# Decode attention with a gated mixer, one core: the main rows of wq requested ahead of its tail, and a root of a constant on ScalarE ahead of the request for x

## The chip, the cores and the metric

The kernel runs on one core of one Trainium2 chip. The metric is the device time of one execution in microseconds (us); lower is better. Times inside an execution are us from the start of the profiled span, and the engines are called as in the profile: PE (TensorE), DVE (VectorE), ACT (ScalarE), POOL (GpSimd), SP (SyncE, which here only requests transfers).

## What is computed

One token of width 448 passes through an attention over a cache of 65536 keys and values, and through a small mixer; a gate blends the two. All inputs are bf16.

```python
D, Hq, Hkv, Sk, Dh, F = 448, 16, 8, 65536, 256, 1792
g = sigmoid((x * gate_w).sum(-1, keepdims=True))
q = (x @ wq).reshape(1, 1, Hq, Dh)                  # wq is [448, 4096]
p = softmax(q . k_cache * Dh ** -0.5)               # two query heads share one of 8 cache heads
a = (p . v_cache).reshape(1, 1, Hq * Dh) @ wo
h = (x - mean(x)) / sqrt(var(x) + 1e-5)
b = gelu(h * w1 + b1) contracted with w2, + b2      # a table of F hidden values for each of D
out = g * a + (1 - g) * b
```

The two caches are 268 MB each. Everything else that is read is under 8 MB.

## The kernel before

**The stream.** The caches are read in 32 blocks (8 heads, 4 blocks of 16384 positions each). A block of keys is 8.39 MB and so is a block of values. A loop with two blocks in each pass handles blocks 0 to 29, and straight code after it handles the last two. Keys lie in `k_all`, which has three slots of half a block; values lie in the single tile `vt`. All large transfers are requested by SP, one after the other, by `load_k_whole` (L132), `load_v` (L135), `load_wo_wide` (L144) and, at the end, `load_v_last`. SP waits in front of a request until its target is free: for the keys of the next block until DVE has transposed the slot (L410), for values until PE has used up the block before (L438). For each block DVE transposes eight pieces of keys, PE multiplies them with the queries (`scores`, L418), the softmax follows, and PE multiplies the weights with the values (`pv`).

**The opening.** Ahead of the loop the queries are made from wq, the mixer is computed as far as its contraction, and constants are built. wq lies for that time in `vt`, where values come later: its rows 0 to 383 as `wq_m` (3 rows to a partition, 3072 KB, called the main rows below), its rows 384 to 447 as `wq_t` (half a row to a partition, 512 KB, the tail). Each column of q takes four matmuls, three with main rows (L299) and one with the tail (L306), so the fourth matmul of 128 needs the tail. The chain of the mixer is: x (`xr`) is spread over the partitions by PE (L245), DVE takes mean and variance (L266 to L269), ACT the root (L272), DVE refines its reciprocal (L275 to L282) and normalises (L283), ACT computes 14 GELUs (L288), PE contracts them (L352). The tables w1, b1, w2 are turned by PE in L263, and DVE copies the result (L273) ahead of the reciprocal. The gate's sum is taken by DVE (L346, L347), and its exponential by ACT (L348). DVE finishes the mixer (L357 to L368), which stands behind the loop in the text and is placed ahead of it by the build. Then all engines meet, and the loop begins: PE spreads a slice of wo and ends a head (L563, L540, L554), DVE adds (L558) and begins to transpose the keys.

**What sets the order.** `seq` fixes the order of instructions on each engine to that of the program's text. Two queues carry transfers: SP's and ACT's. On ACT's queue stand x, the three tables, the gate's weights in two halves, and b2, in this order, ahead of ACT's arithmetic. On SP's queue stand the tail of wq, its main rows and block 0 of the keys.

**The counters.** The build gives each transfer one of eight completion counters, in turn. A transfer that gets a counter which an earlier transfer holds is not requested before that one has landed, and what stands behind it on its queue waits too. Before the change they are: x 0, tail 1, tables 2 to 4, main rows 5, gate halves 6 and 7, b2 again 0 (it waits for x), keys of block 0 again 1 (they wait for the tail).

Of the kernel before, what the change touches and what calls it, by code (L numbers as in the profile page):

```python
# [8 lines left out]
FP32 = mybir.dt.float32  # L9
BF16 = mybir.dt.bfloat16  # L10
ACT = mybir.ActivationFunctionType
# [22 lines left out]
def kernel(  # L34
# [15 lines left out]
    nc = tc.nc  # L50
# [12 lines left out]
    def seq(ins):  # L63
        e = ins.ins.engine
        if e in last:
            tc.add_manual_dep(
                ins.ins,
                last[e],
                mybir.DependencyInfo(
                    mybir.DependencyClass.NoSync, mybir.DependencyReason.DATA  # L70
                ),
                reason="program order",
            )
        last[e] = ins.ins.name
        return ins

    kvpool = ctx.enter_context(tc.tile_pool(name="kvpool", bufs=1))
    const = ctx.enter_context(tc.tile_pool(name="const", bufs=1))
# [26 lines left out]
    xr = const.tile([1, D], BF16)  # L105
# [4 lines left out]
    DM = 384  # L110
    wq_m = vt[:, 0:48, :].rearrange("p a b -> p (a b)").rearrange("p (k n) -> p k n", k=3)
# [47 lines left out]
    def load_v_last(n):  # L159
# [3 lines left out]
                in_=rows("v", n)[:, j0:j1, :],  # L163
            ))

    seq(nc.scalar.dma_start(out=xr[:], in_=A_x[0, 0].rearrange("(o n) -> o n", o=1)))
    seq(nc.sync.dma_start(
        out=wq_t[:, :], in_=A_wq[DM:D, :].rearrange("r (h n) -> (r h) n", h=2)
    ))
    seq(nc.sync.dma_start(out=wq_m, in_=A_wq[0:DM, :].rearrange("(p k) n -> p k n", k=3)))  # L170
    for k, table in enumerate((
        B_w1[0].rearrange("(b p) -> b p", p=128),
        B_b1.rearrange("(b p) -> b p", p=128),
# [3 lines left out]
    for n0, n1 in ((0, D // 2), (D // 2, D)):  # L177
        seq(nc.scalar.dma_start(
            out=gw[:, n0:n1], in_=gate_w.rearrange("(o n) -> o n", o=1)[:, n0:n1]
# [14 lines left out]
        out=val[:], in_=rowsel[:, :, :, 0:NI], op=ALU.add, axis=AXIS.XY  # L194
    ))
    fst = const.tile([128, 2, REP], FP32)
    for e in range(2):
        seq(nc.vector.tensor_reduce(
            out=fst[:, e, :], in_=rowsel[:, :, :, e:e + 1], op=ALU.add, axis=AXIS.XY
# [3 lines left out]
        out=par[:], in_=ident_f[:].rearrange("p (a r) -> p r a", r=REP), op=ALU.add, axis=AXIS.X  # L203
# [3 lines left out]
        out=nval[:], in0=val[:], scalar1=-scale, scalar2=None, op0=ALU.mult  # L207
# [7 lines left out]
        out=same[:], in_=val[:].unsqueeze(1).to_broadcast([128, 64, REP])  # L215
# [8 lines left out]
        out=sel[:],  # L224
        in_=ident.rearrange("p (w k) -> p w k", w=NW).unsqueeze(2).to_broadcast([128, NW, NQ, 32]),
# [7 lines left out]
        out=xrr[:], in_=xr[:, DM:D].unsqueeze(2).to_broadcast([1, D - DM, 2])  # L233
    ))
    x_col = hd_ps[:, 40:44]
    for k in range(3):
# [13 lines left out]
        out=xtm[:], in0=par[:], scalar1=x_col[:, 3:4], scalar2=None, op0=ALU.mult  # L250
# [19 lines left out]
        out=veps[:], in0=mv[:, 1:2], scalar1=1e-5, scalar2=None, op0=ALU.add  # L270
# [5 lines left out]
    for _ in range(2):  # L276
# [3 lines left out]
            out=ntmp[:], in0=ntmp[:], scalar1=-0.5, scalar2=1.5, op0=ALU.mult, op1=ALU.add  # L280
# [3 lines left out]
        out=h_bc, in0=xf, scalar1=mv[:, 0:1], scalar2=rstd[:, 0:1],  # L284
        op0=ALU.subtract, op1=ALU.mult,
    ))
    for b in range(NF):
        seq(nc.scalar.activation(  # L288
            out=gel[b], in_=h_bc, func=ACT.Gelu_apprx_tanh,
# [33 lines left out]
    for k in range(2):  # L323
        seq(nc.vector.tensor_copy(
            out=qq[:, :, :, k, :], in_=qq_ps.rearrange("p (w g r) -> p w g r", g=HKV, r=REP)
# [314 lines left out]
    for n in (L - 1, L):  # L640
# [14 lines left out]
        else:  # L655
            def rest_base():
# [9 lines left out]
                out=lsv[:], in0=val[:], scalar1=lsum[:, 0:1], scalar2=None, op0=ALU.mult  # L666
# [8 lines left out]
                out=rdv[:], in0=rdv[:], scalar1=gcol[:, 0:1], scalar2=None, op0=ALU.mult  # L675
# [6 lines left out]
    for c in range(2):  # L682
# [9 lines left out]
        out=oT[:], in0=o_last, in1=rdv[:].unsqueeze(1).to_broadcast([128, 2, REP]), op=ALU.mult  # L692
# [43 lines left out]
```

## Time and profile before

| what | value |
|---|---|
| device time, median of 3 runs (lowest, highest) | 1264.28 us (1263.87, 1925.72) |
| span of the profiled execution | 1261.8 us |
| moved in the span | 544.36 MB, mean 431 GB/s |
| PE, DVE, ACT busy | 824.5, 711.8, 75.7 us |
| ACT busy in the first of 40 slices of the span | 4 tenths; none in any later slice |

Of the profiled execution the page gives its span; what lies around it is not recorded, and the median of the runs is 2.5 us above the span. A row of the timeline gives start and duration in us, engine, line, operation, tiles, count, and in brackets the idle time of the engine before it and what ended that. SPq and ACTq mark what the sequencers of SP and ACT do, such as requests for transfers. A row of the table by stretches gives the stretch, its length, then for PE, PE's weight load, DVE, ACT and POOL the busy time and the count, then the granted clock of PE, the share of the 16 DMA engines that was busy, and GB/s. Packets are put to the stretch in which they begin, so the share of a short stretch can be over 1.

### The profile page before, as it was taken

What the parts mean: (1) busy time and instruction counts of PE and PEld (TensorE: products, weight loads), DVE (VectorE), ACT (ScalarE), POOL (GpSimd) and SP (SyncE); (2) the same over time, 40 slices, a digit from 0 to 9 for tenths busy, and PEclk for the clock granted to TensorE, in tenths of its full rate; (3) what the DMA queues carried; (4) which work ended last, traced back from release to release, by engine and by line L of the source; (5) the groups of instructions that cost most, each with busy time, mean ns of one, the idle gap of its engine ahead of it and who ended that gap; (6) DMA issues with size and microseconds to landing.
All of it is one profiled execution on the core that took longest, in us unless ns stands there. A gap on an engine that the chain in (4) does not pass through costs nothing.

```text
span 1261.8 us, 12358 instructions
## 1 busy us (share of the span) xinstructions
PE 824.5 (65%) x4818; PEld 331.2 (26%) x4818; DVE 711.8 (56%) x755; ACT 75.7 (6%) x163; POOL 4.8 (0%) x9
## 2 busy tenths in 40 slices
PE   4757467575666756577566766658656576665668
PEld 2222122222222312223222322223222232222224
DVE  5665456654556644566544665445655456654575
ACT  4000000000000000000000000000000000000000
POOL 1000000000000000000000000000000000000000
PEclk8887788877787877978778887788877797877878
DMA  9999999999999999999999999999999999999998
GB/s 415 435 435 432 439 432 432 437 434 437 432 434 435 434 425 440 416 441 443 423 434 437 432 432 439 432 439 432 432 439 432 439 432 432 439 432 435 421 435 355
DMA packets 11624, 544.36 MB, mean 431 GB/s; under 512 B 1532, under 2 KB 1918, under 8 KB 2782
## 3 DMA queue, kind: packets, MB, share of 16 engines
q1 hardware_dynamic: 11522, 544.22, 99.6%
q8 instruction: 6, 0.10, 0.0%
q14 instruction: 4, 0.03, 0.0%
q10 hardware_dynamic: 92, 0.01, 0.0%
HBM read 544.22 MB, written 0.00 MB: 431 GB/s over the span
## 4 chain that ended last, share of the span: by engine, by line
DMA 67%; PE 14%; DVE 13%; issue 4%; ACT 0%; SPq 0%; DVEq 0%; ACTq 0%
DMA k_all<-in_A_k_cache_dram 67%; PE sc L418 13%; DVE kT L410 13%; PE hd_ps L463 0%; PE pv_last L438 0%; PE pv_last L563 0%; PE f L563 0%; DVE rmax L475 0%; PE hd_ps L684 0%; ACT p_sb L506 0%; PE hd_ps L554 0%; PE pv_ps L438 0%; PE f L697 0%; PE sm_ps L493 0%; DVE pT L513 0%
## 5 line engine op out<-in xcount | busy, mean ns | idle before, releaser
L418 PE MATMUL sc<-kT,qz 128*128 128x512 bf16 x2048 | 550.4, 419 | 315.0 <-DVE kT L410 314.8
L410 DVE STREAM_TRANSPOSE kT<-k_all 128x2048 f32<-128x2048 f32 x256 | 571.3, 2283 | 207.6 <-DMA k_all<-in_A_k_cache_dram 154.7
L418 PEld LDWEIGHTS <-qz 128*128 128x128 bf16 x2048 | 212.5, 104 | 651.3 <-issue 474.8
L438 PE MATMUL pv_ps<-vt,pT 128*4 128x512 bf16 x1968 | 172.0, 525 | 27.3 <-DVE pT L513 27.3
L519 DVE SCALAR_TENSOR_TENSOR acc<-acc,al,pv_ps 128x512 f32<-128x512 f32 x31 | 23.2, 747 | 160.4 <-PE pv_ps L438 160.4
L438 PEld LDWEIGHTS <-pT 128*4 128x4 bf16 x2000 | 56.5, 108 | 130.1 <-issue 83.9
L506 ACT ACTIVATE p_sb<-sc,nb 128x512 bf16<-128x512 f32 x32 | 22.0, 687 | 1020.0 <-DVE nb L502 1020.0
L475 DVE TENSOR_REDUCE rmax<-sc 128x1 f32<-128x512 f32 x32 | 22.1, 692 | 63.7 <-PE sc L418 63.7
L513 DVE STREAM_TRANSPOSE pT<-p_sb 128x512 bf16<-128x512 bf16 x32 | 22.8, 712 | 27.1 <-ACT p_sb L506 27.1
L525 PE MATMUL hd_ps<-lsum,same 128*128 128x1 f32 x30 | 8.2, 342 | 28.8 <-DVE lsum L514 28.8
L493 PE MATMUL sm_ps<-mrun,ones_f 1*128 1x2 f32 x64 | 12.1, 256 | 21.2 <-DVE mrun L492 13.0
L479 PE MATMUL sm_ps<-ident_f,rmax 128*1 128x128 f32 x32 | 8.6, 270 | 24.5 <-DVE rmax L475 24.5
L563 PE MATMUL pv_last<-wo_in,steps 128*128 128x448 bf16 x64 | 15.6, 368 | 5.5 <-PEq L605 5.5
L563 PEld LDWEIGHTS <-steps 128*128 128x128 bf16 x128 | 11.6, 101 | 22.6 <-issue 14.4
L493 PEld LDWEIGHTS sm_ps<-mrun,ones_f 1*128 1x128 f32 x64 | 9.4, 182 | 27.4 <-DVE mrun L492 16.3
L567 ACT CAST wo_sb<-pv_last 128x448 bf16<-128x448 f32 x16 | 8.5, 532 | 126.3 <-PE pv_last L563 126.3
L558 DVE TENSOR_TENSOR a_acc<-a_acc,hd_ps 1x448 f32<-1x448 f32 x15 | 9.1, 608 | 12.3 <-PE hd_ps L554 12.3
L554 PE MATMUL hd_ps<-wo_sb,oT 128*1 128x448 bf16 x60 | 15.8, 351 | 0.0
L563 PE MATMUL f<-wo_in,steps 128*128 128x448 bf16 x64 | 15.5, 367 | 0.0
L570 ACT COPY wo_sb<-wo_sb 128x896 bf16<-128x896 bf16 x15 | 14.1, 937 | 14.5 <-PE hd_ps L554 14.5
L525 PEld LDWEIGHTS hd_ps<-lsum,same 128*128 128x128 f32 x30 | 6.9, 285 | 30.1 <-DVE lsum L514 30.1
L550 DVE CAST oT<-hd_ps 128x2 bf16<-128x2 f32 x15 | 2.4, 160 | 20.8 <-PE hd_ps L540 20.8
(124 smaller groups left out, 194.6 us busy)
## 6 DMA issues: line engine op xcount, KB each, us to landing
k_all<-in_A_k_cache_dram SPq DMA_DIRECT2D x2, 4096.0 KB, 15.2
vt<-in_A_v_cache_dram SPq DMA_DIRECT2D x1, 5120.0 KB
k_all<-in_A_v_cache_dram SPq DMA_DIRECT2D x1, 4096.0 KB
wo_in<-in_A_wo_dram SPq DMA_DIRECT2D x15, 224.0 KB, 27.8
vt<-in_A_wq_dram SPq DMA_DIRECT2D x1, 3072.0 KB, 10.4
vt<-in_A_v_cache_dram SPq DMA_DIRECT2D x1, 3072.0 KB
k_all<-in_A_v_cache_dram SPq DMA_DIRECT2D x1, 2048.0 KB
k_all<-in_A_v_cache_dram SPq DMA_DIRECT2D x1, 1024.0 KB, 21.7
```

The costliest lines, as they stand in the source:

```text
L410: seq(nc.vector.transpose(out=kT_tiles[i % 2][:].rearrange("p j w k c -> p (j w k c)").bitcast(FP32), in_=slots[pair[i // 4]][:, i % 4 * N ...
L418: seq(nc.tensor.matmul(sc_tiles[e][:, :], lhsT=qz[:, 2 * w + c, 2 * (NI - i):2 * (NI - i) + 128], rhs=kT_tiles[i % 2][:, :, w, :, c], star ...
L438: seq(nc.tensor.matmul(dst[32 * grp:32 * grp + 2 * REP, :, :], lhsT=pT[:, 32 * jj + 2 * REP * ip:32 * jj + 2 * REP * (ip + 1)], rhs=pairs( ...
L475: seq(nc.vector.tensor_reduce(out=rmax[:], in_=sc_ps[:, :], op=ALU.max, axis=AXIS.X))
L493: seq(nc.tensor.matmul(sm_ps[:, 128:128 + REP], lhsT=ones_f[0:1, :], rhs=mrun[0:1, :], start=True, stop=True))
L506: seq(nc.scalar.activation(out=p_sb[:, :], in_=sc_ps[:, :], func=ACT.Exp, scale=scale, bias=nb[:, 0:1], accum_out=den[:, 0:1],))
L513: seq(nc.vector.transpose(out=pT[:, :], in_=p_sb[:, :]))
L519: seq(nc.vector.scalar_tensor_tensor(out=acc[:], in0=acc[:], scalar=al_tiles[e][:, 0:1], in1=src[:, :, :], op0=ALU.mult, op1=ALU.add,))
L525: seq(nc.tensor.matmul(hd_ps[:, 460:461], lhsT=same[:].rearrange("p a r -> p (a r)"), rhs=lsum[:, 0:1], start=True, stop=True,))
L554: seq(nc.tensor.matmul(a_ps, lhsT=oT[:, c, r:r + 1], rhs=wo_sb[:, r, c, :], start=(r == 0 and c == 0), stop=(r == REP - 1 and c == 1),))
L563: seq(nc.tensor.matmul(wo_ps[c], lhsT=steps[:, WS - u:WS - u + 128], rhs=wo_in[:, 2 * u + c, :], start=(u == 0), stop=(u == WS - 1),))
L570: seq(nc.scalar.copy(out=wo_sb[:, 0], in_=wo_sb[:, 1]))
```

## The change

The request for the main rows goes ahead of that for the tail on SP. On ACT, a root of a constant 1.0 is taken ahead of the first request; DVE sets the constant, as its first instruction.

```diff
-    seq(nc.scalar.dma_start(out=xr[:], in_=A_x[0, 0].rearrange("(o n) -> o n", o=1)))
+    seq(nc.sync.dma_start(out=wq_m, in_=A_wq[0:DM, :].rearrange("(p k) n -> p k n", k=3)))
     seq(nc.sync.dma_start(
         out=wq_t[:, :], in_=A_wq[DM:D, :].rearrange("r (h n) -> (r h) n", h=2)
     ))
-    seq(nc.sync.dma_start(out=wq_m, in_=A_wq[0:DM, :].rearrange("(p k) n -> p k n", k=3)))
+    warm = const.tile([1, 1], FP32)
+    seq(nc.vector.memset(warm[:], 1.0))
+    seq(nc.scalar.activation(out=warm[:], in_=warm[:], func=ACT.Sqrt))
+    seq(nc.scalar.dma_start(out=xr[:], in_=A_x[0, 0].rearrange("(o n) -> o n", o=1)))
     for k, table in enumerate((
```

In the built program ACT's first load of the root's table moves with the new root to the head of ACT's instructions, and no load is left ahead of L272. The number of table loads stays three. The counters come out as: main rows 0, x 1, tables 2 to 4, gate halves 5 and 6, b2 7, tail again 0, keys of block 0 again 1. So the first three requests of SP stand like this, with what each waits for:

```
before                                        after
tail of wq                                    main rows of wq
main rows of wq                               tail of wq         [waits for counter 0: the main rows]
keys of block 0 [waits for counter 1: tail]   keys of block 0    [waits for counter 1: x]
```

All other instructions of PE, DVE, POOL and SP keep their order.

## The prediction

> **What bounds the kernel now.** I read the page's head first, then the table by stretches, then the chain of waits, and last the timeline of the opening, where the change lies.
>
> ```profile
> span 1261.8 us, 12358 instructions
> DMA  9999999999999999999999999999999999999998
> ...
> 51.00:1200.00 1149.00, 746.72 (x4201) 296.24 (x4199) 636.68 (x653) 57.92 (x134) 0.00 (x0) 0.81 1.00 434
> 1200.00:1250.00 50.00, 39.11 (x198) 15.09 (x201) 38.85 (x28) 1.41 (x4) 0.00 (x0) 0.85 1.00 431
> 1250.00:1261.80 11.80, 8.96 (x206) 6.10 (x194) 3.33 (x9) 0.85 (x4) 0.00 (x0) 0.75 0.60 244
> ```
>
> All 16 DMA engines are busy from the opening until some 5 us before the end: share 1.00 and 434 GB/s over 1149 us, 1.00 and 431 over the next 50. No compute engine comes near (PE 746.72 of 1149). So the time is the bytes at 434 GB/s, plus what comes before the first byte and after the last. A stop in that stream is made up nowhere; an engine's delay costs something only if a request then comes after the queue has run dry.
>
> The chain of waits shows the same link as a latency, and must not be read as one:
>
> ```profile
> 43.98 26.68 DMA k_all<-in_A_k_cache_dram
> ...
> 0.74 0.42 SPq L167 DMA_DIRECT2D vt<-in_A_wq_dram  x1
> ...
> 1.22 0.41 SPq L170 DMA_DIRECT2D vt<-in_A_wq_dram  x1
> ...
> 3.98 0.33 SPq L132 DMA_DIRECT2D k_all<-in_A_k_cache_dram  x1
> 27.07 0.35 SPq L135 DMA_DIRECT2D vt<-in_A_v_cache_dram  x1
> ...
> vt<-in_A_v_cache_dram SPq DMA_DIRECT2D x1, 24.3
> ...
> DMA to landing us min/median/max: 26.7/27.4/28.1
> ```
>
> The last row is of the key requests in the first 60 us: there are two, and the one at 43.98 has the 26.68, so the one at 3.98 has the 28.1 and block 0 lands at 32.1. The values requested at 27.07 land at 27.07 + 24.3 = 51.4. The keys requested at 43.98 land at 70.7; their 8.39 MB take 8.39 / 0.434 = 19.3 us, and 51.4 + 19.3 = 70.7. So they did not travel for 26.68 us, they stood in line behind the values for 7.4 of them. Requests in the loop have about 7 us of slack.
>
> **The change part by part. The tail's wait on SP.** Tail and main rows were asked for back to back, and the keys as soon as the tail had landed, with the main rows still on their way. Now the tail waits for the main rows, through counter 0, and the keys stand behind it on SP. When the main rows have landed nothing large is queued, and the DMA engines stand still until the tail's first bytes.
>
> ```profile
> vt<-in_A_wq_dram SPq DMA_DIRECT2D x1, 3072.0 KB, 10.4
> ...
> vt<-in_A_wq_dram SPq DMA_DIRECT2D x1, 512.0 KB, 3.2
> ...
> 1.50:1.75 0.25, 0.00 (x0) 0.00 (x0) 0.00 (x0) 0.00 (x0) 0.25 (x1) 1.00 0.01 4
> 1.75:2.00 0.25, 0.00 (x0) 0.00 (x0) 0.00 (x0) 0.00 (x0) 0.23 (x1) 1.00 0.61 213
> ...
> 4.00:5.00 1.00, 0.00 (x0) 0.00 (x0) 1.00 (x1) 1.00 (x1) 1.00 (x1) 1.00 0.96 397
> ...
> 6.00:7.00 1.00, 0.22 (x3) 0.13 (x2) 0.89 (x5) 0.00 (x0) 0.00 (x0) 1.00 0.98 397
> ```
>
> The tail, requested at 0.74, took 3.2 us. Its 0.524 MB at 434 GB/s are 1.2 of them, so 2.0 are fixed: about 1.0 to the first bytes (share 0.01 up to 1.75, 0.61 after), the rest from the last byte to the landing. Before, main rows and tail had both landed at 1.22 + 10.4 = 11.6. Now the main rows are asked for at 0.74 and have no tail ahead of them, so they land 1.2 earlier, at 10.4; the tail is asked for then and lands 3.2 later, at 13.6. That is 2.0 later for the same bytes. The keys are asked for one request behind (1.22 - 0.74 = 0.5), at 10.9; their first bytes would be there at 11.9, before the tail's are through, so no second hole opens. From there on the stream is the old one, 2.0 later: block 0 lands at 34.1, the values behind it at 53.4. That term is the forecast.
>
> The Trainium skill, page DMA: Bandwidth & Descriptors, section Specifications, gives about 0.6 us to the first byte for requests from Sync or Scalar. The rows above show 1.0, and the trace decides; by the page's figure the hole would be an estimated 0.4 shorter and the sum 1.6.
>
> The hole has no row of its own in this trace. Its lower bound: only the 1.0 to the first bytes shows, and the main rows, alone, run at 434 instead of the 397 they had beside the small transfers (3.146 / 0.397 - 3.146 / 0.434 = 0.7 back), so 0.3. Its upper bound: all 3.2 of the tail, if the main rows land no earlier than before. I take 2.0, which the tail's own row gives; the start from rest is the same there.
>
> **What waits for the later tail and keys.**
>
> ```profile
> 11.69 0.24 PE L299 MATMUL hd_ps<-xm,vt 128*128 128x1 bf16 x3 [1.47 <-DMA vt<-in_A_wq_dram]
> ...
> 15.30 0.19 DVE L314 CAST qb<-hd_ps 128x32 bf16<-128x32 f32 x1 [2.55 <-PE hd_ps L306]
> ...
> 19.76 0.61 DVE L347 TENSOR_REDUCE z<-k_all 1x1 f32<-1x448 f32 x1
> 22.03 1.28 ACT L348 ACT_TABLE_LOAD   x1
> ...
> 25.30 0.61 DVE L368 TENSOR_TENSOR rest<-y_sb,rest 1x448 f32<-1x448 f32 x1
> ...
> 32.82 4.49 DVE L410 STREAM_TRANSPOSE kT<-k_all 128x2048 f32<-128x2048 f32 x2
> ```
>
> PE makes three matmuls from the main rows at 10.4 and then holds at L306 until 13.6, with everything of PE behind it: 128 matmuls that began at 11.69 now run 1.9 later. DVE is held at L314 from 15.30 to 17.2, and its rows up to L347 follow: the sum that ended at 20.37 ends at 22.3. ACT's load for the exponential waits for it and started at 22.03 anyway, so 0.3 reaches L368, the loop's entry, and the request for the values: 27.07 becomes 27.4. Block 0 is still arriving then, so the queue never sees it. The first transpose moves from 32.82 to 34.1, when its keys land, 1.3 later; the next request for keys follows, 43.98 to 45.3, still 8 us ahead of the values' landing at 53.4.
>
> **The root and the queue of ACT.**
>
> ```profile
> 0.74 0.53 ACTq L166 DMA_DIRECT2D xr<-in_A_x_dram  x1
> ...
> 2.03 0.10 PEld L237 LDWEIGHTS <-xr 1*128 1x128 bf16 x1 [2.03 <-DMA xr<-in_A_x_dram]
> 2.13 0.41 ACTq L176 DMA_DIRECT2D tables<-in_B_w_dram  x1
> ...
> 2.33 3.07 DVE L190 CAST ident_f<-steps 128x128 f32<-128x128 bf16 x1 [2.33 <-POOL steps masks.py:199]
> ...
> 3.75 1.28 ACT L272 ACT_TABLE_LOAD   x1 [3.75 <-issue]
> ...
> 6.38 0.22 PE L237 MATMUL hd_ps<-ones_b,xr 1*128 1x1 bf16 x3 [6.38 <-DVE ones_b L212]
> ...
> 10.00 0.10 PEld L263 LDWEIGHTS <-tables 42*128 42x128 bf16 x1 [1.96 <-issue]
> ...
> 10.26 0.20 ACT L272 ACTIVATE sdev<-veps 128x1 f32<-128x1 f32 x1 [5.23 <-DVE veps L269]
> ```
>
> The table load only changes its place: it ended at 5.03, and ACT then idled 5.23 us until DVE had the variance, so taking it away from there saves nothing. At the head of ACT it and the root push all seven small requests back by 1.28 + 0.20, about 1.5: x goes out at 2.2, b2 last at about 5. DVE's new first instruction falls into the 2.33 us in which DVE waits for POOL: nothing.
>
> x took 2.03 - 0.74 = 1.3, on an idle path, and is not needed before 6.38, when DVE has made the ones. Requested at 2.2 it lands at 3.5 if nothing is in its way. Something is: the main rows now begin first. The bound from above is the tables, which went out beside the main rows: requested until 2.54, and L263, which waits for them, could load at 10.00. The worst is that x comes when the main rows are through, at 10.4; then PE starts 4.0 late, and so at most do the mixer, the loop's entry and the request for the values, 31.1 instead of 27.07. Its first bytes would come at 32.1, while block 0 has bytes until about 34.1 - 1.0 = 33.1. Even this worst case leaves no hole; the cover is block 0's own 19 us. I take zero.
>
> **Sum.** +2.0 for the hole, 0 for the rest: 1261.8 + 2.0 = 1263.8 of span. What lies around the profiled span isn't given; the median is 2.5 above it and I leave that as it is: 1264.28 + 2.0 = 1266.3.
>
> **Rivals.**
> *The chain is a latency after all.* Then what counts is the first transpose, 1.3 later, with every landing a fixed time behind its request, and the end is 1.3 later: 1265.6. Against it: 51.4 + 19.3 = 70.7.
> *Not slower.* The opening's arithmetic, not the stream, sets when the loop begins to matter: the chain of waits does run through compute from 26 to 44 us, and block 0 (32.1) was there ahead of its transpose (32.82). If the table load were on that path, 1.28 would come off it, and the main rows' start at 10.4 instead of 11.69 would help: 1264.28 - 1.28 = 1263.0. It decides if the root waits for its table and the values' request meets an empty queue. Both fail here: 5.23 us of idle time ahead of the root, 5 us of block 0 left at 27.07. The Trainium skill, page ScalarE: Activation LUTs, section What ACT_TABLE_LOAD costs, puts a switch of tables at 2.66 us with a drain; by that an estimated 1261.6 in this rival. The rows show 1.28, then a wait for DVE.
> *Clearly slower: the values come to a dry queue.* x and then the tables are each held until the main rows are through, one after the other. Beyond the 4.0 above, the request would have to slip another 1.0 (33.1 - 32.1), and every further us is paid in full: the tables' latency again, 10.00 - 2.54 = 7.5, would give 1266.3 + 6.5 = 1272.8. Against it: the small packets got through beside the main rows before, and the hole itself is free for them.
> *The change doesn't do what it says:* the main rows do go first, but the fourth matmul of q needs the tail, so nothing of q comes earlier. This is part of the forecast.
>
> **How the numbers follow.** Forecast 0.84, latency 0.05, not slower 0.05, dry queue 0.03; 0.03 for something I don't see. The range takes the bounds of the hole, 0.3 and 3.2, and 0.4 of scatter (1264.28 against the lowest run, 1263.87) on both sides: 1264.2 to 1267.9. It holds the forecast and the latency case and leaves out the others, 0.11. Two per cent are 25 us, about what a measurement tells from no change; that would need 0.8 us in each of 32 blocks, while the requests of the loop have 7 us of slack: slower 0.02, faster 0.01, within 0.97.
>
> **What would show it.** In the profile of the changed kernel: one or two stretches of 1 us with hardly any DMA between 9 and 12 us, and none before; SP's second request at about 10.4 and its third 0.5 later; L306 held until about 13.6; the first transpose at about 34.1, released by the keys; the request for the values still within 1 us of 27.4; 434 GB/s in the long stretch; a span of about 1263.8. Wrong would be: SP's second request soon after its first, a first transpose still at 32.8, a share under 1 around 33 us, or an x that comes after 6.4 and moves L237.

## The result

The changed kernel takes 1266.77 us (median of 16 runs, 1266.22 to 1267.60), the kernel before 1264.04 us over its 16 runs beside them: 2.73 us more, a ratio of 1.0021 with a 95% interval of 1.0014 to 1.0027, or 1.8 to 3.4 us. Two runs of the kernel before, at 1925.72 and 1566.17 us, lie far above all others and are left out of the ratio. The forecast was 1266.3, +2.0.

The profiled execution of the changed kernel took 1267.14 us, with a span of 1265.3; so 1.8 us lie around a span, not the 2.5 that I had left standing. The head of its page and three stretches answer to those shown of before:

```profile
span 1265.3 us, 12361 instructions
DMA  9999999999999999999999999999999999999998
...
51.00:1200.00 1149.00, 745.13 (x4209) 296.24 (x4208) 638.34 (x653) 57.92 (x134) 0.00 (x0) 0.81 1.00 434
1200.00:1250.00 50.00, 35.81 (x163) 13.92 (x162) 37.81 (x23) 0.96 (x3) 0.00 (x0) 0.83 0.99 424
1250.00:1265.30 15.30, 11.85 (x235) 7.31 (x233) 4.55 (x14) 1.30 (x4) 0.00 (x0) 0.87 0.68 279
```

The long stretch is the old one: share 1.00, 434 GB/s. What was added lies outside it. The requests of SP in the changed kernel, with the times to landing of the two parts of wq, and the table by stretches around the second request:

```profile
0.73 0.42 SPq L166 DMA_DIRECT2D vt<-in_A_wq_dram  x1
11.04 0.33 SPq L167 DMA_DIRECT2D vt<-in_A_wq_dram  x1
11.42 0.42 SPq L132 DMA_DIRECT2D k_all<-in_A_k_cache_dram  x1
28.03 0.35 SPq L135 DMA_DIRECT2D vt<-in_A_v_cache_dram  x1
46.20 0.34 SPq L132 DMA_DIRECT2D k_all<-in_A_k_cache_dram  x1
```

```profile
vt<-in_A_wq_dram SPq DMA_DIRECT2D x1, 3072.0 KB, 10.3
vt<-in_A_wq_dram SPq DMA_DIRECT2D x1, 512.0 KB, 3.2
```

```profile
9.00:10.00 1.00, 0.00 (x0) 0.00 (x0) 0.93 (x3) 0.00 (x0) 0.00 (x0) 1.00 0.70 297
10.00:11.00 1.00, 0.00 (x0) 0.00 (x0) 0.19 (x2) 0.73 (x2) 0.00 (x0) 1.00 0.02 3
11.00:12.00 1.00, 0.41 (x4) 0.34 (x4) 0.65 (x5) 0.76 (x1) 0.00 (x0) 1.00 0.00 0
12.00:13.00 1.00, 0.00 (x0) 0.00 (x0) 0.79 (x7) 0.00 (x0) 0.00 (x0) 1.00 0.96 254
```

The tail is requested at 11.04, when the main rows have landed, and the keys right behind it. The trace also holds a record of every packet, with its start, duration and bytes; below these are called the packet records, and a packet's bytes are spread evenly over its duration where they are added up. By them the last packets of the main rows begin before 10 and are through by 10.7, and the first of the tail begins at 12.0. In between hardly a byte moves: that is the hole. Main rows and tail have both landed at 11.04 + 3.2 = 14.2 instead of 11.6, so 2.6 later, and that is nearly the whole 2.73. Block 0 of the keys follows, and the chain of waits and DVE's timeline show it landing and being taken up:

```profile
11.42 23.62 DMA k_all<-in_A_k_cache_dram
...
46.20 27.57 DMA k_all<-in_A_k_cache_dram
...
35.07 4.50 DVE L413 STREAM_TRANSPOSE kT<-k_all 128x2048 f32<-128x2048 f32 x2
```

It lands at 35.0 instead of 32.1 (the forecast was 34.1), and the first transpose starts right then. Added up from the packet records, the stream is 0.3 us behind that of the kernel before at 10 us, ahead of the hole, and 2.9 behind from 20 to 60 us.

### The profile page after: what moved, and what is told of

It reads as the page before. It is cut to its first block, busy times and chain, and to the rows that moved or that the text cites. A ratio compares the mean times of both kernels' runs of the same rounds, so it can differ in the third digit from the quotient of the medians.

```text
span 1265.3 us, 12361 instructions
## 1 busy us (share of the span) xinstructions
PE 821.2 (65%) x4818; PEld 331.5 (26%) x4818; DVE 711.5 (56%) x756; ACT 75.9 (6%) x164; POOL 4.8 (0%) x9
## 4 chain that ended last, share of the span: by engine, by line
DMA 71%; DVE 13%; PE 12%; issue 4%; SPq 0%; ACT 0%; DVEq 0%
DMA k_all<-in_A_k_cache_dram 69%; DVE kT L413 12%; PE sc L421 12%; DMA k_all<-in_A_v_cache_dram 2%; DMA vt<-in_A_wq_dram 1%; SPq L161 0%; PE f L700 0%; ACT p_sb L509 0%; DVE rmax L478 0%; SPq L132 0%; PE sm_ps L496 0%; DVE res L706 0%; DVEq L413 0%; SPq L167 0%; PE sm_ps L482 0%
## 5 line engine op out<-in xcount | busy, mean ns | idle before, releaser
L566 PEld LDWEIGHTS <-steps 128*128 128x128 bf16 x128 | 11.6, 101 | 22.4 <-issue 14.1
L496 PEld LDWEIGHTS sm_ps<-mrun,ones_f 1*128 1x128 f32 x64 | 9.4, 182 | 27.4 <-DVE mrun L495 16.3
## 6 DMA issues: line engine op xcount, KB each, us to landing
vt<-in_A_wq_dram SPq DMA_DIRECT2D x1, 3072.0 KB, 10.3
```

Source lines behind the costliest of these rows:

```text
L496: seq(nc.tensor.matmul(sm_ps[:, 128:128 + REP], lhsT=ones_f[0:1, :], rhs=mrun[0:1, :], start=True, stop=True))
L566: seq(nc.tensor.matmul(wo_ps[c], lhsT=steps[:, WS - u:WS - u + 128], rhs=wo_in[:, 2 * u + c, :], start=(u == 0), stop=(u == WS - 1),))
```

## The experiments

All times are medians beside runs of the kernel before on the same chip. The diffs are against the kernel named.

**The order alone.** Against the changed kernel:

```diff
-    warm = const.tile([1, 1], FP32)
-    seq(nc.vector.memset(warm[:], 1.0))
-    seq(nc.scalar.activation(out=warm[:], in_=warm[:], func=ACT.Sqrt))
```

> The main rows of wq go first, without the root; x is again the first thing on ACT. The counters come out so that the tail still waits for the main rows. Theory (the time is the hole between the main rows' landing and the tail's first bytes, plus a slower start of the stream when its first packets are 24 KB instead of 4 KB): SP's second request at 10.8 to 11.1, the tail's landing at 14.0 to 14.3, 1266.6 us. Rival (the root at the head of ACT pays a part, because x comes at 5.1 instead of 2.0 and its packet holds up one DMA engine): second request at 10.4, 1266.0 us. Rival (order costs nothing, the root does it all): 1264.0 us.

Measured: 1265.62 against 1264.04, ratio 1.0014 (1.0005 to 1.0023). No theory met it, because the expectation had the waits wrong. Without the root, counter 0 goes to x and 1 to the main rows: the tail waits for x, and the keys wait for the main rows. SP's requests and two stretches of this run show it:

```profile
2.43 0.33 SPq L167 DMA_DIRECT2D vt<-in_A_wq_dram  x1
10.97 0.33 SPq L132 DMA_DIRECT2D k_all<-in_A_k_cache_dram  x1
...
10.00:11.00 1.00, 0.00 (x0) 0.00 (x0) 0.19 (x2) 0.73 (x2) 0.00 (x0) 1.00 0.90 366
11.00:12.00 1.00, 0.23 (x3) 0.23 (x4) 0.34 (x3) 0.76 (x1) 0.00 (x0) 1.00 0.72 254
```

The tail's 512 KB still run while SP learns of the main rows' landing, and so fill most of the hole: +1.6 instead of +2.7. It is the same hole, partly covered; some 0.45 of the 1.6 stays without any wait, as the third run shows.

**The root alone.** Against the kernel before:

```diff
+    warm = const.tile([1, 1], FP32)
+    seq(nc.vector.memset(warm[:], 1.0))
+    seq(nc.scalar.activation(out=warm[:], in_=warm[:], func=ACT.Sqrt))
     seq(nc.scalar.dma_start(out=xr[:], in_=A_x[0, 0].rearrange("(o n) -> o n", o=1)))
```

> The root is added, the order of SP stays tail, main rows, keys. By the build's counters (tail 0, main rows 1, x 2, tables 3 to 5, gate 6 and 7, b2 0, keys 1) the keys now wait for the main rows instead of the tail, so there is a hole between main rows and keys although no request changes its place. Theory: the keys are requested at 11.7 instead of 3.98, the hole is 2.0 (the fixed part of a request), +2.0 to +2.4, 1266.0 to 1266.4 us. Rival (the order is what costs and the root is free): 1264.0 us.

Measured: 1266.41 against 1264.04, ratio 1.0019 (1.0010 to 1.0028), as the theory had it. A root on ACT that nothing waits for costs 2.4 us, through the counters: tail and main rows go out at 0.73 and 1.22 as before, but the keys now hold counter 1 after the main rows.

```profile
11.58 0.33 SPq L132 DMA_DIRECT2D k_all<-in_A_k_cache_dram  x1
...
11.00:12.00 1.00, 0.40 (x15) 0.39 (x15) 0.81 (x6) 0.76 (x1) 0.00 (x0) 1.00 0.01 0
12.00:13.00 1.00, 1.00 (x44) 1.00 (x42) 0.82 (x6) 0.00 (x0) 0.00 (x0) 1.00 2.69 918
```

**The whole change without a wait.** Against the changed kernel:

```diff
-    for n0, n1 in ((0, D // 2), (D // 2, D)):
+    for n0, n1 in ((0, D),):
...
-    seq(nc.scalar.dma_start(out=b2b[:], in_=B_b2.rearrange("(o n) -> o n", o=1)))
     load_k_whole(0, 0)
+    seq(nc.sync.dma_start(out=b2b[:], in_=B_b2.rearrange("(o n) -> o n", o=1)))
```

> The changed kernel (main rows first, root first), with the gate's weights in one request instead of two and b2 requested by SP behind the keys. That leaves seven requests ahead of the keys, and neither the tail nor the keys wait for a counter. Theory: all three requests of SP go out in the first 2 us, no hole, and what is left is the slow start with 24 KB packets, 0.4: 1264.4 us, block 0 landing at 32.5. Rival (the order or the root costs by itself, whatever waits): 1266.8 us. Rival (the hole is everything, the start costs nothing): 1264.0 us, block 0 at 32.1.

Measured: 1264.49 against 1264.04, ratio 1.0003 (0.9994 to 1.0012). Order and root are the changed kernel's; only the waits are gone, and with them 2.3 of the 2.7 us. Its requests on SP, and the two stretches in which the changed kernel stood still:

```profile
0.73 0.41 SPq L166 DMA_DIRECT2D vt<-in_A_wq_dram  x1
1.20 0.41 SPq L167 DMA_DIRECT2D vt<-in_A_wq_dram  x1
1.67 0.42 SPq L132 DMA_DIRECT2D k_all<-in_A_k_cache_dram  x1
...
10.00:11.00 1.00, 0.00 (x0) 0.00 (x0) 0.18 (x2) 0.74 (x2) 0.00 (x0) 1.00 1.21 499
11.00:12.00 1.00, 0.27 (x4) 0.28 (x4) 0.37 (x4) 0.75 (x1) 0.00 (x0) 1.00 2.46 1057
```

**The root in the old order, without a changed wait.** Against the run with the root alone; the keys wait for the tail again.

```diff
-    for n0, n1 in ((0, D // 2), (D // 2, D)):
+    for n0, n1 in ((0, D),):
```

> The root in the old order, with the gate's weights in one request, so that the keys wait for the tail as before. Theory: the root and x's later place cost nothing without a changed wait: keys requested at about 4.0, 1264.0 us. Rival (root and table load ahead of the small requests cost by themselves, through later tables and a later loop): 1264.7 to 1265.5 us.

Measured: 1264.21 against 1264.04, ratio 1.0001 (0.9992 to 1.0010). The first two requests for keys:

```profile
4.19 0.33 SPq L132 DMA_DIRECT2D k_all<-in_A_k_cache_dram  x1
...
46.15 0.34 SPq L132 DMA_DIRECT2D k_all<-in_A_k_cache_dram  x1
```

The root itself costs nothing that stands out of the noise. The second of these requests comes 2.17 later than in the kernel before (43.98), because the loop starts later, and the end does not follow it.

**A longer hole.** Against the kernel before:

```diff
-    wq_t = vt[:, 48:56, :].rearrange("p a b -> p (a b)")
+    wq_t = slots[0][:, 0:8, :].rearrange("p a b -> p (a b)")
...
-    load_k_whole(0, 0)
...
+    load_k_whole(0, 0)
     qb = work.tile([128, 2 * HQ], BF16)
```

> The kernel before, with the tail of wq laid into the first slot of the keys, so that block 0 of the keys cannot be requested before PE has made its last product with the tail: a hole of about 4 us more than any so far, nothing else moved. Theory (a hole in the stream costs its own length, once): keys requested at 15.4, block 0 landing 23.1 later as in the run with the root alone, at 38.5 instead of 32.1, and 6.2 to 6.4 more at the end: 1270.3 us. Rival (the 7 us of slack of the loop's requests take up part of a late start): 1266 to 1267 us.

Measured: 1270.23 against 1263.88, ratio 1.0050 (1.0037 to 1.0064), so +6.35. The request for the keys, and the chain of waits behind it:

```profile
15.45 0.33 SPq L132 DMA_DIRECT2D k_all<-in_A_k_cache_dram  x1
...
15.45 22.46 DMA k_all<-in_A_k_cache_dram
...
13.00:16.00 3.00, 2.72 (x96) 2.60 (x94) 0.19 (x1) 3.00 (x5) 0.00 (x0) 1.00 0.02 5
...
51.00:1200.00 1149.00, 740.78 (x4209) 294.85 (x4207) 639.93 (x652) 56.86 (x132) 0.00 (x0) 0.81 1.00 434
```

Block 0 lands at 37.9 instead of 32.1, 5.8 later, and the end is 6.35 later. The landings differ by less than the end because in the kernel before one packet of block 0 came late (it ends at 31.57, those of the other engines by 30.65); by the packet records the stream is 6.2 behind at 60 us and still 6.2 at 100. It gives nothing back: 434 GB/s again.

**The loop later by 2.6 and by 9.2 us.** Against the changed kernel, with `(0, 1, 2, 3, *range(NF))` in the first run and `(*range(NF), *range(NF))` in the second:

```diff
-    for b in range(NF):
+    for b in (0, 1, 2, 3, *range(NF)):
         seq(nc.scalar.activation(
             out=gel[b], in_=h_bc, func=ACT.Gelu_apprx_tanh,
```

> The changed kernel with 4 of the 14 GELUs of the opening made twice, so that the loop and the request for the first values come 2.6 us later, at 30.7 instead of 28.0. Theory (the opening's arithmetic is hidden behind block 0 of the keys, whose packets run until 33): 1266.8 us, as the changed kernel. Rival (the loop's entry sets the time, and so part of the change's cost came through it): 1269.4 us.

Measured: 1266.95, against 1266.77 of the changed kernel; beside this run and the next the kernel before took 1263.88, where it took 1264.04 beside the changed kernel. The ratio is 1.0025 (1.0016 to 1.0035), against 1.0021 (1.0014 to 1.0027). The request for the values, and the second block of keys in the chain of waits:

```profile
30.65 0.35 SPq L135 DMA_DIRECT2D vt<-in_A_v_cache_dram  x1
...
48.87 24.68 DMA k_all<-in_A_k_cache_dram
```

The values are requested at 30.65 instead of 28.03, which costs nothing that stands out of the noise. The second block of keys is requested 2.67 later than in the changed kernel (46.20) and lands no later: 48.87 + 24.68 = 73.6 against 46.20 + 27.57 = 73.8.

> The changed kernel with all 14 GELUs made twice: request for the first values 9.2 us later, at 37.3, first bytes at 38.3. Theory: now the queue runs dry when block 0 is through, at about 33.3 on most DMA engines, so a hole of 5.0 and a slow start of up to 0.4 are added to the changed kernel's 1266.8: 1271.8 to 1272.2 us. Rival (no cover: every us of the opening counts): 1276.0 us. Rival (the loop's slack takes it up): 1266.8 us.

Measured: 1271.96, ratio 1.0063 (1.0049 to 1.0077), 5.2 above the changed kernel. Request and stretches of this run:

```profile
36.63 0.35 SPq L135 DMA_DIRECT2D vt<-in_A_v_cache_dram  x1
...
34.00:35.00 1.00, 0.00 (x0) 0.00 (x0) 0.80 (x2) 0.00 (x0) 0.00 (x0) 1.00 0.00 0
35.00:36.00 1.00, 0.00 (x0) 0.00 (x0) 0.31 (x1) 0.00 (x0) 0.00 (x0) 1.00 0.00 0
36.00:37.00 1.00, 0.30 (x1) 0.13 (x2) 0.00 (x0) 0.00 (x0) 0.00 (x0) 1.00 0.06 16
37.00:38.00 1.00, 1.00 (x4) 0.45 (x3) 0.00 (x0) 0.00 (x0) 0.00 (x0) 1.00 2.85 918
```

Here the queue does run dry, and 8.6 us of later request become 5.2 of later end. So the opening's arithmetic has at least some 3.4 us of cover in the changed kernel (8.6 - 5.2), and inside it costs nothing. It is rather more, since the 5.2 also hold a slow start: by the packet records 15 of the 16 engines are through with block 0 by 33.2, the first packet of the values begins at 37.62, and the values' first packets take 2.9 to 3.5 us where later ones of 64 KB take 2.42.

**Why the first request for main rows is slow.** Three runs without any hole. The first is the run without a wait, with

```diff
-    seq(nc.sync.dma_start(out=wq_m, in_=A_wq[0:DM, :].rearrange("(p k) n -> p k n", k=3)))
+    mp = A_wq[0:DM, :].rearrange("(p k) n -> p k n", k=3)
+    seq(nc.sync.dma_start(out=wq_m[:, 0:1, 0:2048], in_=mp[:, 0:1, 0:2048]))
+    seq(nc.sync.dma_start(out=wq_m[:, 0:1, 2048:], in_=mp[:, 0:1, 2048:]))
+    seq(nc.sync.dma_start(out=wq_m[:, 1:3], in_=mp[:, 1:3]))
```

> As the run without waits (main rows first, gate's weights in one request, b2 on SP behind the keys), but the first of a partition's three main rows is requested in two halves, packets of 4 KB, and the other two rows in one request behind, packets of 16 KB. The tail waits for the first half, which lands at about 4 while the rest is on its way, so no hole. Theory (packets of 24 KB into a resting stream start slowly, 230 GB/s in the first 3 us against 306 with 4 KB): back to about 300 GB/s there, 1264.0 to 1264.2 us. Rival (the order, not the packet size, makes the slow start): 230 GB/s again, 1264.5 us.

The second is the run with the root in the old order and no changed wait, with the tail's layout given to rows 0 to 63:

```diff
-        out=wq_t[:, :], in_=A_wq[DM:D, :].rearrange("r (h n) -> (r h) n", h=2)
+        out=wq_t[:, :], in_=A_wq[0:D - DM, :].rearrange("r (h n) -> (r h) n", h=2)
...
-    seq(nc.sync.dma_start(out=wq_m, in_=A_wq[0:DM, :].rearrange("(p k) n -> p k n", k=3)))
+    seq(nc.sync.dma_start(out=wq_m, in_=A_wq[D - DM:D, :].rearrange("(p k) n -> p k n", k=3)))
```

with x split to match. 

> As the run with the root in the old order and free counters, but the 64 rows in the tail's layout are the first of wq (rows 0 to 63) and the main rows are 64 to 447. The first request is again 512 KB that lie in one piece in memory, 4 KB to a partition, only elsewhere. Theory after the last runs (a stream that starts with neighbouring 4 KB pieces starts quickly, one that starts with pieces 24 KB apart slowly): 306 GB/s in the first 3 us after 1 us, 1264.0 to 1264.2 us. Rival (the tail's place in memory is what makes it quick): 230 GB/s, 1264.5 us.

The third is again the run without a wait, with

```diff
+    mp = A_wq[0:DM, :].rearrange("(k p) n -> p k n", k=3)
+    seq(nc.sync.dma_start(out=wq_m[:, 0:1], in_=mp[:, 0:1]))
+    seq(nc.sync.dma_start(out=wq_m[:, 1:3], in_=mp[:, 1:3]))
```

in place of the one request for main rows, and x read in the same order. 

> As the run without waits, main rows first, but partition p holds rows p, 128 + p and 256 + p instead of three neighbours, and row p is requested first: 1 MB in one piece, 8 KB to a partition; the other two rows follow in one request. Theory (distance of the first pieces in memory makes the slow start): about 300 GB/s in the first 3 us after 1 us, 1264.1 us. Rival (the first request for main rows starts slowly in any layout): 230 GB/s or less, 1264.5 us.

Measured: 1264.46, 1264.13 and 1264.43, against 1263.88, 1263.90 and 1263.90. The first 3 us of the stream, from each run's table by stretches, in this order: the kernel before, the changed kernel, main rows in 4 KB pieces, first rows as tail, rows in line.

```profile
1.00:4.00 3.00, 0.00 (x0) 0.10 (x1) 1.67 (x1) 0.25 (x1) 2.98 (x3) 1.00 0.78 306
```

```profile
1.00:4.00 3.00, 0.00 (x0) 0.00 (x0) 1.67 (x1) 1.23 (x2) 2.97 (x3) 1.00 0.84 246
```

```profile
1.00:4.00 3.00, 0.00 (x0) 0.10 (x1) 1.68 (x1) 1.23 (x2) 2.97 (x3) 1.00 0.68 187
```

```profile
1.00:4.00 3.00, 0.00 (x0) 0.10 (x1) 1.68 (x1) 1.23 (x2) 2.97 (x3) 1.00 0.79 306
```

```profile
1.00:4.00 3.00, 0.00 (x0) 0.09 (x1) 1.67 (x1) 1.22 (x2) 2.98 (x3) 1.00 0.75 227
```

Every kernel whose first request is the 512 KB in the tail's layout has 306 GB/s there, wherever they lie in memory; every kernel that begins with main rows has less, in pieces of 4, 8 or 24 KB, 24 KB apart or in one piece. A packet counts where it begins, so large packets look better in this table than they are. Added up from the packet records, which do not have this fault, the stream is at 5 us between 0.25 and 0.5 behind that of the kernel before in all seven kernels that begin with main rows, and at most 0.12 behind in the four others that begin with the tail's layout. So the slow start is there in the packets. The tail's place fell as a cause, and so did packet size and distance, each by itself; that neighbouring rows take up a part is possible (rows in line has the 0.25) and not shown. What is left, that the tail's layout starts well, is no cause. The three kernels that begin with main rows and have no hole stand 0.45, 0.58 and 0.53 above the kernel before; the two that begin with the tail's layout and have none stand 0.17 and 0.23 above it. Each of these intervals holds no change; the difference of some 0.3 in time between the two groups rests on five medians.

## Why the prediction was right, and where it was off

**The stream bounds the kernel, and a stop in it is made up nowhere.** Shown: 434 GB/s in the long stretch of the changed kernel and of the run with the long hole, in which the stream is 6.2 us behind at 60 us and the end comes 6.35 later. The rival in which the chain of waits is a latency would have had the first transpose's delay as the end's. The first transpose moved from 32.82 to 35.07, 2.25, and the end by 2.73; this run alone does not part the two, and the long hole hardly does, with transposes that move 5.1 and an end that moves 6.35. Two other runs do. With the root in the old order the first transpose starts at 34.75, 1.93 later than in the kernel before, and the end moves by 0.17. With 4 GELUs twice it starts at 37.48, 2.41 later than in the changed kernel, the next request for keys follows 2.67 later, and the end moves by 0.18. In both it is the start of the loop that holds the transpose, not the keys, and the queue takes up the later request. So the chain is no latency, as the prediction argued from 51.4 + 19.3 = 70.7.

**The tail's wait makes a hole.** Shown by the run without waits, which has the changed order and the root and loses only 0.45. The Trainium skill, page DMA: Bandwidth & Descriptors, section Anatomy of one DMA — SWDGE (gpsimd) path, which is written for requests from GpSimd, says that DMA engines don't wait on semaphores and that a wait is spent on the issuing sequencer before dispatch; the trace agrees for SP, with SP's second request at 11.04 and the keys, which wait for nothing by then, 0.38 behind it.

**The size of the hole: 2.0 forecast, 2.6 in the rows, 2.73 in the time.** The interval of the time, 1.8 to 3.4, holds 2.0 as well; that the hole was longer is read from the rows. The fixed part of a request was right as a sum: the tail took 3.2 again, and its first packets came at 12.0, about 1.0 after the request, as in the row of before. What the prediction called the rest, "from the last byte to the landing", was read wrong. In the kernel before the tail's packets begin at 1.79 and the last ends at 3.62, by the packet records, and it lands at 3.9: only some 0.3 lie behind the last byte, and the 0.524 MB took 1.8 from rest instead of 1.2. The changed kernel has the same (12.00, 13.92, 14.2), so the sum of 2.0 held.

The Trainium skill, page DMA: Bandwidth & Descriptors, section Specifications, has about 0.6 to the first byte. The 1.0 is counted from the start of SP's request. Counted from its end, 0.74 + 0.42 = 1.16 in the kernel before and 11.04 + 0.33 = 11.37 in the changed one, the first packets come 0.63 later in both, so the traces do not contradict the page. The hole contains the request itself, and 1.0 is the right term for it.

The term that was mis-sized is "they land 1.2 earlier, at 10.4": they landed at 11.0. The step took off the tail's bytes at the rate of the running stream, and so gave the main rows the tail's quicker start as well ("the start from rest is the same there"). At the head of SP they take 10.3 us from request to landing, where 9.7 was reckoned. The bounds of 0.3 and 3.2 held it.

**The root and ACT's queue: zero forecast, zero found, but by another way.** The requests were to go out 1.5 later, behind table load and root. They did not:

```profile
0.74 1.28 ACT L172 ACT_TABLE_LOAD   x1 [0.74 <-PEq L723]
...
0.91 0.52 ACTq L173 DMA_DIRECT2D xr<-in_A_x_dram  x1
...
2.03 0.20 ACT L172 ACTIVATE warm<-warm 1x1 f32<-1x1 f32 x1
...
5.10 0.10 PEld L240 LDWEIGHTS <-xr 1*128 1x128 bf16 x1 [5.10 <-DMA xr<-in_A_x_dram]
...
11.03 0.10 PEld L266 LDWEIGHTS <-tables 42*128 42x128 bf16 x1 [2.99 <-issue]
...
14.29 0.19 PE L309 MATMUL hd_ps<-xtm,vt 128*128 128x1 bf16 x1 [2.47 <-DMA vt<-in_A_wq_dram]
```

x was requested at 0.91, while the table was still loading, and landed at 5.1 all the same, because the main rows were ahead of it. With the tail ahead instead, in the run with the root alone, x was requested at 0.90 and had landed by 2.88:

```profile
2.88 0.10 PEld L240 LDWEIGHTS <-xr 1*128 1x128 bf16 x1 [2.88 <-DMA xr<-in_A_x_dram]
```

The 5.1 lies between the 3.5 and the 10.4 that were given, and before the 6.38 at which it is needed. The tables came at least 1.0 later than before (11.03, where they had landed by 10.00), and the mixer, the loop's entry and the request for the values with them: 28.03, not 27.4. The run with the loop 2.6 later shows that this costs nothing. The fourth matmul of q waited for the tail until 14.29, as foreseen, 0.7 later than 13.6 because the tail was.

**The rivals.** Latency: it fell by the two runs named above. Not slower: it fell, the root's load saves nothing (root in the old order, 1264.21). Dry queue: it did not happen, but the mechanism is real; the run with all GELUs twice shows it at 36.63. What I had not listed is that root and order each make a hole alone. The sum put all of it on the order; the counters tie the two together, and which request waits for which comes out differently in each of the four kernels.

## What to carry to other kernels

Where completion counters are handed out in turn, adding an instruction that costs nothing or changing the order of requests can make a late request wait for an early large one; look in the built program at what the first large requests wait for, before thinking of durations. In a kernel whose DMA engines are always busy, price a stop by the fixed part of a request in its own trace (its time to landing less its bytes at the stream's rate), add some tenths of a us for a start from rest, and expect every other change of the opening to cost nothing while a transfer still runs (here 2.6 us cost nothing, 8.6 us did cost). Fewer requests ahead of the large ones (here the gate's weights in one piece, and b2 behind the keys) took the wait away.

## What the runs showed of the hardware that was not expected

Requests for transfers on ACT's queue go out while ACT loads a table: 0.91 against a load from 0.74 to 2.02. And a stream that starts from rest is slower than its later rate. In the half microsecond from 2.5 the changed kernel begins no packet at all, since its first ones are still under way, and the kernel before runs at 401 GB/s:

```profile
2.50:3.00 0.50, 0.00 (x0) 0.00 (x0) 0.50 (x1) 0.00 (x0) 0.50 (x1) 1.00 0.00 0
```

```profile
2.50:3.00 0.50, 0.00 (x0) 0.00 (x0) 0.50 (x1) 0.00 (x0) 0.50 (x1) 1.00 0.98 401
```

Keys requested into a resting stream at 15.45 took 22.46 us to land, of which 19.3 are their bytes at 434 GB/s and 2.0 the fixed part; 1.2 are left over. By the packet records its first packets of 64 KB take some 3 us where later ones take 2.42. Why 512 KB in the tail's layout escape most of this stays open.
